# Routing of an attention-then-experts kernel: one product on TensorE, one copy on ScalarE and one merged operation in place of five on GpSimd

## Chip, cores and metric

The kernel runs on one core of a Trainium2 chip. The metric is the device time of one execution in microseconds (us), of which the median of three runs is taken. PE is TensorE's matmul, PEld its weight load, DVE VectorE, ACT ScalarE, POOL GpSimd, SP SyncE.

## What is computed

Four batches of 12288 queries attend to 768 pooled keys each, and each of the 49152 results goes through a gate: a skip score decides whether it is sent to an expert at all, and the largest of eight logits says to which. Cut from the reference:

```python
s = scale * (q @ k.transpose(0, 2, 1))
a = np.exp(s - s.max(-1, keepdims=True)); a /= a.sum(-1, keepdims=True) + 1e-09
x = (a @ v).reshape(B * S, D)
do_compute = x @ w_skip > 0
xc = x[do_compute]
logits = xc @ w_gate
e_idx = np.argmax(logits, axis=1)
gate_w = probs[np.arange(len(xc)), e_idx]        # softmax of the logits
y[mask] = gate_w[mask, None] * (np.maximum(xc[mask] @ w1[e], 0.0) @ w2[e])
out[do_compute] = xc + y
```

## The kernel before, in words

**Two phases.** Phase 1 (until about 1050 us) is attention: 384 tiles of 128 queries, in one loop over t whose order is written out by hand (every engine executes its instructions in the order in which the loop emits them). Phase 2 (from about 1090 us) is the experts, a hardware loop of four steps of 512 rows. Between them a few expert steps are peeled off and woven into the last tiles.

**One tile of phase 1.** TensorE makes the scores of tile t (lines 595 to 597), the weighted sum of tile t-6 (L658) and two transposes of tile t-1 (L633). VectorE takes the row maximum (L603, `nm`), ScalarE the exponential (L608, `p_sb`) and a float16 high part (L612), VectorE the low part (L616). On every second tile VectorE also makes the reciprocal `rs` of the row sums (L666, L668), which empties an accumulator in PSUM that TensorE needs again; ScalarE then scales the rows into the tile `rows` (L673), and SyncE stores them. GpSimd makes the low half of the queries (`q_lo`, L577) and, while batches 0 to 2 run, pools the keys of the batch after (`kvt`, L437 and L440). The last batch has no batch after it, so there these pooling steps are missing.

**Routing.** Every 12 tiles a generator `route` (from L679) is started for the 12x128 rows just finished; 31 of them work for GpSimd (`eng` is GpSimd), and the last 12 tiles are routed in three parts of four tiles by VectorE (`few`). A route is advanced by one step per tile, so its parts lie between the work of the tiles that follow. Its parts, by line:
- L705 to L709: the logits, their maximum and the differences `d`; L721, L722: the position of the maximum; L723: `act`, 1 for a row with a positive skip score; L724, L725: `na`, a large number beyond all rows of the scratch array for an inactive row, 0 for an active one.
- Some tiles later: L733, the exponential `ex` on ScalarE; L735, L737, L738: the one-hot matrix `oh_all` of the chosen expert, with a column of zeros ahead of the 12 tiles of each expert.
- L745: the sum `gs` on VectorE; L765, L766: two products on TensorE into one PSUM tile `misc`, the totals per tile and expert and the counts of the rows above.
- L769: a scan on VectorE, from 0 for each expert, makes running totals `pre` of the 12 tiles; L772 adds the counts inside a tile. On GpSimd L773 makes `nxt`, the totals that the next route starts from, L774 the gate's denominator `gs`, L775 adds the totals `run` that this route started from, L777 selects the expert's column.
- One tile later: L779, VectorE's reciprocal of `gs`, which waits for L774. Then L785, L787: the row number `di`; L788, L789 on GpSimd: the row's scale is copied into column C+2 of `rows`, its number into column C+1; then 12 scatters (L183, one per tile of the route, spread over the tiles that follow) write the rows into the experts' lists in `scr`.

After the last scatter SyncE loads expert rows from `scr` (L189), and phase 2 can begin.

Of the kernel before, what the change touches and what calls it, by code (L numbers as in the profile page):

```python
# [9 lines left out]
F32 = mybir.dt.float32  # L10
# [5 lines left out]
ALU = mybir.AluOpType  # L16
# [4 lines left out]
RT = 12  # L21
# [3 lines left out]
def kernel(  # L25
# [11 lines left out]
    nc = tc.nc  # L37
    NR, C, RT, P = q.shape
# [7 lines left out]
    E, _, FF = w1.shape  # L46
# [32 lines left out]
    BIG = 1 << 20  # L79
# [13 lines left out]
    ones_bf = consts.tile([P, P], BF16, name="ones_bf")  # L93
# [5 lines left out]
    ones_f = consts.tile([P, P], F32, name="ones_f")  # L99
# [10 lines left out]
                            op0=ALU.mult, op1=ALU.add)  # L110
    idt_i = consts.tile([P, RT], I32, name="idt_i")
    nc.gpsimd.iota(idt_i, pattern=[[1, RT]], base=BIG, channel_multiplier=RT)
    idt = consts.tile([P, RT], F32, name="idt")
    nc.gpsimd.tensor_copy(idt, idt_i)

    ends = consts.tile([P, E], F32, name="ends")
# [4 lines left out]
    RTP = RT + 1  # L121
# [44 lines left out]
    op = ctx.enter_context(tc.tile_pool(name="op", bufs=2))  # L166
# [15 lines left out]
    def scatter_rows(dst, ids, src, bound, group):  # L182
        ins = nc.gpsimd.indirect_dma_start(  # L183
            out=dst, out_offset=bass.IndirectOffsetOnAxis(ap=ids, axis=0), in_=src, in_offset=None,
            bounds_check=bound, oob_is_err=False).ins
        return no_dep(ins, group)
# [178 lines left out]
    with ExitStack() as p1:  # L365
# [10 lines left out]
        rt = p1.enter_context(tc.tile_pool(name="rt", bufs=3))  # L376
# [7 lines left out]
        def misc_ps():  # L384
            return ps_m.tile([P, 512], F32, name="misc") if started else acc_ps()
# [161 lines left out]
        accs, scales, snaps = {}, [], []  # L547
# [138 lines left out]
        def route(r, a, b, last, eng):  # L686
            n = b - a
            rows = ROWS[r][:, a:b, :]
            L = rt.tile([P, RT, E], F32, name="lg")[:, 0:n, :]
            S3 = [P, n, E]  # L690
            x_sc = KV[r * RT // TPB][5]

            def small_t(name, dt=F32):
                return rt.tile([P, RT], dt, name=name)[:, 0:n]

            def big_t(name, dt=F32):
                return rt.tile([P, RT, E], dt, name=name)[:, 0:n, :]

            def bc(x):
                return x.unsqueeze(2).broadcast_to(S3)  # L700

            def em(x):
                return x.unsqueeze(1).broadcast_to(S3)

            nc.vector.tensor_tensor(out=L, in0=rows[:, :, C + 1:C + 1 + E], in1=em(gate_ds[:, 1:1 + E]), op=ALU.mult)  # L705
            mx = small_t("mx")
            nc.vector.tensor_reduce(out=mx, in_=L, axis=AX.X, op=ALU.max)
            d = big_t("d")
            eng.tensor_tensor(out=d, in0=L, in1=bc(mx), op=ALU.subtract)  # L709
            ev = big_t("ev")  # L710
            act = small_t("act")
            na = small_t("na")
            few = eng is nc.vector
            if few:
                eng.scalar_tensor_tensor(out=ev, in0=d, scalar=0.0, in1=em(em8), op0=ALU.is_equal, op1=ALU.mult)
                eng.tensor_scalar(out=act, in0=rows[:, :, C], scalar1=0.0, scalar2=None, op0=ALU.is_gt)
                eng.scalar_tensor_tensor(out=na, in0=rows[:, :, C], scalar=0.0, in1=idt[:, 0:n], op0=ALU.is_le,
                                         op1=ALU.mult)
                ohb = oh_few[a // GT % 2]
            else:  # L720
                eng.tensor_scalar(out=ev, in0=d, scalar1=0.0, scalar2=None, op0=ALU.is_equal)  # L721
                eng.tensor_tensor(out=ev, in0=ev, in1=em(em8), op=ALU.mult)  # L722
                eng.tensor_scalar(out=act, in0=rows[:, :, C], scalar1=0.0, scalar2=None, op0=ALU.is_gt)  # L723
                eng.tensor_scalar(out=na, in0=act, scalar1=-1.0, scalar2=1.0, op0=ALU.mult, op1=ALU.add)  # L724
                eng.tensor_tensor(out=na, in0=na, in1=idt[:, 0:n], op=ALU.mult)  # L725
                oha = oh_all[r % 3]
                ohb = oha.rearrange("p e t -> p t e")[:, 1:RTP, :]
            yield
            if not few:
                for _ in range(3 if r < LASTR - 1 else K1):  # L730
                    yield
            ex = big_t("ex")
            nc.scalar.activation(out=ex, in_=d, func=AF.Exp)  # L733
            mn = small_t("mn")
            nc.vector.tensor_reduce(out=mn, in_=ev, axis=AX.X, op=ALU.min)  # L735
            oh = big_t("oh")
            nc.vector.tensor_tensor(out=oh, in0=em(em8), in1=bc(mn), op=ALU.is_equal)  # L737
            eng.tensor_tensor(out=ohb[:, 0:n, :], in0=oh, in1=bc(act), op=ALU.mult)  # L738
            for _ in range(1 if few else 2 if r < LASTR - 1 else K2):
                yield  # L740
            yield (None if r >= LASTR - 1 else GT - 1)
            while accs.get("done", 0) != r * RT + a:
                yield (None if r >= LASTR - 1 else GT - 1)
            gs = small_t("gs")
            nc.vector.tensor_reduce(out=gs, in_=ex, axis=AX.X, op=ALU.add)  # L745
            ps = misc_ps()
            w = n * E
            acc = big_t("acc")
            nxt = ends if last else rt.tile([P, E], F32, name="nxt")
            run = accs.get("run", base0)  # L750
            accs["run"] = nxt
            if few:
                ohf = ohb.rearrange("p t e -> p (t e)")
                nc.tensor.matmul(ps[:, 0:w + E], upper_bf, ohf[:, 0:w + E], start=True, stop=False)
                for j in range(n):
                    nc.tensor.matmul(ps[:, (j + 1) * E:w + E], ones_bf,
                                     ohb[:, j:j + 1, :].broadcast_to([P, n - j, E]), start=False, stop=(j == n - 1))
                nc.vector.tensor_tensor(out=nxt, in0=run, in1=ps[:, w:w + E], op=ALU.add)
                nc.vector.tensor_tensor(out=acc, in0=ps[:, 0:w].rearrange("p (t e) -> p t e", e=E), in1=em(run),
                                        op=ALU.add)  # L760
                nc.vector.tensor_scalar(out=gs, in0=gs, scalar1=1e-9, scalar2=x_sc, op0=ALU.add, op1=ALU.mult)
            else:
                wa = E * RTP
                ohf = oha.rearrange("p e t -> p (e t)")
                nc.tensor.matmul(ps[:, 0:wa], ones_bf, ohf, start=True, stop=True)  # L765
                nc.tensor.matmul(ps[:, wa:2 * wa], upper_bf, ohf, start=True, stop=True)  # L766
                yield
                pre = rt.tile([P, E, RTP], F32, name="pre")
                nc.vector.tensor_tensor_scan(pre.rearrange("p e t -> p (e t)"), keep.rearrange("p e t -> p (e t)"),  # L769
                                             ps[:, 0:wa], 0.0, ALU.mult, ALU.add)  # L770
                inner = ps[:, wa:2 * wa].rearrange("p (e t) -> p t e", t=RTP)[:, 1:RTP, :]
                nc.vector.tensor_tensor(out=acc, in0=inner, in1=pre.rearrange("p e t -> p t e")[:, 0:RT, :], op=ALU.add)  # L772
                eng.tensor_tensor(out=nxt, in0=run, in1=pre[:, :, RT], op=ALU.add)  # L773
                eng.tensor_scalar(out=gs, in0=gs, scalar1=1e-9, scalar2=x_sc, op0=ALU.add, op1=ALU.mult)  # L774
                eng.tensor_tensor(out=acc, in0=acc, in1=em(run), op=ALU.add)  # L775
            accs["done"] = r * RT + b
            eng.tensor_tensor(out=acc, in0=acc, in1=ohb[:, 0:n, :], op=ALU.mult)  # L777
            yield
            nc.vector.reciprocal(rows[:, :, C], gs)  # L779
            yield  # L780
            if r == SNAPR:
                snapshot(accs["run"])
                yield
            dest = small_t("dest")
            nc.vector.tensor_reduce(out=dest, in_=acc, axis=AX.X, op=ALU.add)  # L785
            di = small_t("di", I32)
            nc.vector.tensor_tensor(out=di, in0=dest, in1=na, op=ALU.add)  # L787
            nc.gpsimd.tensor_copy(rows[:, :, C + 2], x_sc.broadcast_to([P, n]))  # L788
            nc.gpsimd.iota(rows.bitcast(I32)[:, :, C + 1], pattern=[[1, n]], base=r * RT * P + a, channel_multiplier=RT)  # L789
            for j in range(n):  # L790
                if j > 0 and r < LASTR - 1 and (j % 2 == 0 or r < SNAPR):
                    yield
                scatter_rows(scr, di[:, j:j + 1], rows[:, j, 0:ROW], E * CAP - 1, "scr")
            if r == SNAPR:
                first_writes.extend(writes)
# [129 lines left out]
        t = -1  # L925
# [138 lines left out]
```

## Time and profile before

| | us |
|---|---|
| median of 3 runs | 1857.39 (1856.57 to 1858.85) |
| the profiled execution, device time | 1859.96 |
| its span, first to last instruction | 1857.0 |
| PE busy | 1752.5 (94%) |
| DVE busy | 1555.6 (84%) |
| ACT busy | 1324.9 (71%) |
| POOL busy | 1144.1 (62%) |
| mean granted clock of TensorE | 0.987 |

The shares are averages over two phases with different limits. Matmuls are pipelined and their ends modelled, so a PE that counts as busy need not be at its peak. "Idle before, releaser" in the rows below is the idle time of an engine ahead of an instruction and what ended it; "issue" is time in which it waited for nothing that the profile shows. Instructions of the sequencers, such as waits and the issue of a DMA, are not counted as busy.

### The profile page before, as it was taken

How to read it: one execution, taken by the hardware profiler on the slowest of the kernel's cores; microseconds unless marked ns; L12 is line 12 of the kernel's file. 1: busy time of each engine (PE TensorE's matmuls, PEld its weight loads, DVE VectorE, ACT ScalarE, POOL GpSimd, SP SyncE). 2: the span in 40 equal slices, each digit the busy share in tenths (PEclk: the TensorE clock that was granted, in tenths of full speed). 3: DMA queues.
4: the chain of work that ended last, by engine and by line, in shares of the span. 5: the costliest groups of instructions: out<-in, count | busy, mean ns of one | idle time of the engine just before them, and what ended most of it. 6: DMA issues, size and time to landing. Idle time of an engine off the chain costs nothing. (4 is left out here: it accounts for less than half of the span.)

```text
span 1857.0 us, 42898 instructions
## 1 busy us (share of the span) xinstructions
PE 1752.5 (94%) x13955; PEld 1260.6 (68%) x13955; DVE 1555.6 (84%) x3226; ACT 1324.9 (71%) x2484; POOL 1144.1 (62%) x1466
## 2 busy tenths in 40 slices
PE   4999999999999999999998879999999999999997
PEld 2998889888889888899998534444444444444443
DVE  7888889988889888998999768887887788778875
ACT  2887788787778787888887546666666666666664
POOL 2378887989978998878778553333333333433343
PEclk9999999999999999999999989999999999999998
DMA  6999999999989999999999443333333333333342
GB/s 179 205 210 201 211 188 216 210 188 175 174 169 198 197 207 204 190 219 221 224 222 188 103 115 98 97 94 93 102 93 94 96 99 93 94 93 102 93 113 73
DMA packets 621971, 284.87 MB, mean 153 GB/s; under 512 B 503168, under 2 KB 571904, under 8 KB 621824
## 3 DMA queue, kind: packets, MB, share of 16 engines
q1 hardware_dynamic: 600320, 244.56, 65.0%
q0 software_dynamic: 21504, 38.43, 6.9%
q8 instruction: 82, 1.34, 0.3%
q14 instruction: 65, 0.53, 0.1%
HBM read 90.60 MB, written 78.64 MB: 91 GB/s over the span
## 5 line engine op out<-in xcount | busy, mean ns | idle before, releaser
L183 POOL DMA_INDIRECT out_dram<-o,xin x288 | 295.3, 1025 | 481.1 <-DVE o L292 414.6
L183 POOL DMA_INDIRECT scr<-rows,di x384 | 413.2, 1076 | 103.3 <-issue 83.3
L269 DVE SCALAR_TENSOR_TENSOR h_lo<-h_ps,h_hi 128x512 f16<-128x512 f32 x544 | 344.2, 686 | 145.8 <-ACT h_hi L268 145.8
L608 ACT ACTIVATE p_sb<-s_ps,nm 128x768 f32<-128x768 f32 x384 | 347.2, 904 | 156.0 <-DVE nm L603 150.4
L603 DVE TENSOR_REDUCE nm<-s_ps 128x1 f32<-128x768 f32 x384 | 363.5, 947 | 54.8 <-PE s_ps L597 53.1
L268 ACT ACTIVATE h_hi<-h_ps 128x512 f16<-128x512 f32 x544 | 318.5, 597 | 51.4 <-PE h_ps L267 31.8
L658 PE MATMUL acc_ps<-v_hi,pt 128*128 128x138 f16 x3072 | 323.2, 225 | 30.3 <-DVE rs L666 30.3
L658 PEld LDWEIGHTS <-pt 128*128 128x128 f16 x4608 | 278.6, 98 | 97.3 <-issue 96.4
L616 DVE SCALAR_TENSOR_TENSOR p<-p_sb,p 128x512 f16<-128x512 f32 x384 | 303.1, 789 | 2.8 <-ACT p L612 2.2
L658 PE MATMUL acc_ps<-v_lo,pt 128*128 128x138 f16 x1536 | 295.9, 224 | 0.0
L595 PE MATMUL s_ps<-k_hi,q_hi 128*128 128x384 f32 x768 | 295.6, 385 | 0.0
L596 PE MATMUL s_ps<-k_lo,q_hi 128*128 128x384 f32 x768 | 261.1, 340 | 0.0
L597 PE MATMUL s_ps<-k_hi,q_lo 128*128 128x384 f32 x768 | 260.2, 339 | 0.0
L612 ACT ACTIVATE p<-p_sb 128x512 f16<-128x512 f32 x384 | 243.2, 633 | 12.6 <-DMA pt<-p 9.3
L265 PE MATMUL h_ps<-xT,w_hi 128*128 128x512 f16 x544 | 206.9, 380 | 8.2 <-issue 8.2
L266 PE MATMUL h_ps<-xT,w_hi 128*128 128x512 f16 x544 | 206.9, 380 | 0.0
L267 PE MATMUL h_ps<-xT,w_lo 128*128 128x512 f16 x544 | 206.7, 380 | 0.0
L281 PE MATMUL y_ps<-h_hi,w_hi 128*128 128x512 f16 x544 | 206.2, 379 | 0.0
L281 PE MATMUL y_ps<-h_hi,w_lo 128*128 128x512 f16 x544 | 206.2, 379 | 0.0
L281 PEld LDWEIGHTS <-w_hi 128*128 128x128 f16 x1152 | 112.7, 98 | 132.6 <-issue 0.7
L284 ACT ACTIVATE yT<-y_ps,y_sc 128x512 f32<-128x512 f32 x68 | 46.8, 688 | 218.3 <-PE y_ps L281 218.3
L281 PE MATMUL y_ps<-h_lo,w_hi 128*128 128x512 f16 x544 | 195.1, 379 | 0.0
(215 smaller groups left out, 3231.3 us busy)
## 6 DMA issues: line engine op xcount, KB each, us to landing
kvt<-in_kv_dram SPq DMA_DIRECT2D x96, 256.0 KB
q_sb<-in_q_dram SPq DMA_DIRECT2D x96, 256.0 KB
out_dram<-rows SPq DMA_DIRECT2D x96, 256.0 KB
xin<-scr SPq DMA_DIRECT2D x75, 264.0 KB, 2.9
w_raw<-in_moe_w_dram SPq DMA_DIRECT2D x38, 512.0 KB, 4.2
scr<-pad SPq DMA_DIRECT2D x32, 264.0 KB
pt<-p SPq DMA_TRANSPOSE x384
scr<-rows,di POOLq DMA_INDIRECT x384
```

The costliest lines, as they stand in the source:

```text
L183: ins = nc.gpsimd.indirect_dma_start(out=dst, out_offset=bass.IndirectOffsetOnAxis(ap=ids, axis=0), in_=src, in_offset=None, bounds_check= ...
L268: nc.scalar.activation(out=h["hi"][:, c, :], in_=ps, func=AF.Relu)
L269: nc.vector.scalar_tensor_tensor(out=h["lo"][:, c, :], in0=ps, scalar=0.0, in1=h["hi"][:, c, :], op0=ALU.max, op1=ALU.subtract)
L281: nc.tensor.matmul(ps, w[:, c, :], h[x][:, c, :], start=(i == 0), stop=(i == len(terms) - 1))
L595: nc.tensor.matmul(s[:, h, :HK], q_hi, k_hi[:, sl], start=True, stop=False)
L596: nc.tensor.matmul(s[:, h, :HK], q_hi, k_lo[:, sl], start=False, stop=False)
L597: nc.tensor.matmul(s[:, h, :HK], q_lo, k_hi[:, sl], start=False, stop=True)
L603: nc.vector.tensor_reduce(out=NM[t], in_=S_PS[t][:, :, :HK], axis=AX.XY, op=ALU.max, negate=True)
L608: nc.scalar.activation(out=P_SB[t], in_=S_PS.pop(t)[:, :, :HK], func=AF.Exp, bias=NM.pop(t))
L612: nc.scalar.activation(out=P16[t][:, 0, :], in_=p_flat(t)[:, 0:KD * P], func=AF.Copy, scale=2.0 ** PEXP)
L616: LO[:] = [nc.vector.scalar_tensor_tensor(out=p16[:, 1, :], in0=p_flat(t)[:, 0:KD * P], scalar=2.0 ** PEXP, in1=p16[:, 0, :], op0=ALU.mult ...
L658: nc.tensor.matmul(ps[:, j % 2, :], w, v[a][:, k, :], start=(i == 0), stop=(i == len(AVL) - 1))
```

## The change

The running totals `run` are no longer added by GpSimd after the scan. A third product on TensorE, one row of ones by one row of eight totals in float32, adds them into the empty column of each expert ahead of the scan, so that `pre` already holds them and its last column is what the next route starts from; L773 and L775 go. `na` becomes one operation with two constants instead of two with a table (an inactive row's number is then the same large constant for all rows). The copy into column C+2 moves from GpSimd, just ahead of the scatters, to ScalarE, just behind `ex`; this one part also holds for the three routes on VectorE.

```diff
                 eng.tensor_scalar(out=act, in0=rows[:, :, C], scalar1=0.0, scalar2=None, op0=ALU.is_gt)
-                eng.tensor_scalar(out=na, in0=act, scalar1=-1.0, scalar2=1.0, op0=ALU.mult, op1=ALU.add)
-                eng.tensor_tensor(out=na, in0=na, in1=idt[:, 0:n], op=ALU.mult)
+                eng.tensor_scalar(out=na, in0=act, scalar1=-float(BIG), scalar2=float(BIG), op0=ALU.mult, op1=ALU.add)
...
             nc.scalar.activation(out=ex, in_=d, func=AF.Exp)
+            nc.scalar.copy(rows[:, :, C + 2], x_sc.broadcast_to([P, n]))
...
-            nxt = ends if last else rt.tile([P, E], F32, name="nxt")
             run = accs.get("run", base0)
-            accs["run"] = nxt
             if few:
+                nxt = ends if last else rt.tile([P, E], F32, name="nxt")
+                accs["run"] = nxt
...
-                nc.tensor.matmul(ps[:, 0:wa], ones_bf, ohf, start=True, stop=True)
+                nc.tensor.matmul(ps[:, 0:wa], ones_bf, ohf, start=True, stop=False)
+                nc.tensor.matmul(ps[:, 0:wa].rearrange("p (e t) -> p e t", t=RTP)[:, :, 0], ones_f[0:1, :], run[0:1, :],
+                                 start=False, stop=True)
                 nc.tensor.matmul(ps[:, wa:2 * wa], upper_bf, ohf, start=True, stop=True)
+                pre = rt.tile([P, E, RTP], F32, name="pre")
+                accs["run"] = pre[:, :, RT]
                 yield
-                pre = rt.tile([P, E, RTP], F32, name="pre")
...
-                eng.tensor_tensor(out=nxt, in0=run, in1=pre[:, :, RT], op=ALU.add)
                 eng.tensor_scalar(out=gs, in0=gs, scalar1=1e-9, scalar2=x_sc, op0=ALU.add, op1=ALU.mult)
-                eng.tensor_tensor(out=acc, in0=acc, in1=em(run), op=ALU.add)
...
             nc.vector.tensor_tensor(out=di, in0=dest, in1=na, op=ALU.add)
-            nc.gpsimd.tensor_copy(rows[:, :, C + 2], x_sc.broadcast_to([P, n]))
             nc.gpsimd.iota(rows.bitcast(I32)[:, :, C + 1], pattern=[[1, n]], base=r * RT * P + a, channel_multiplier=RT)
```

## Rows read from the trace of the kernel before

**Rows 1.** The page, busy tenths of GpSimd in 40 slices of the span.

```profile
POOL 2378887989978998878778553333333333433343
```

**Rows 2.** Stretches of phase 1: PE, PEld, DVE, ACT, POOL busy (count); clock, DMA share, GB/s.

```profile
325.00:516.00 191.00, 177.63 (x1908) 163.67 (x1906) 167.55 (x312) 152.21 (x281) 171.84 (x234) 0.99 0.96 186
828.00:942.00 114.00, 114.00 (x1249) 106.14 (x1247) 104.43 (x208) 99.62 (x184) 92.49 (x124) 1.00 1.14 227
```

**Rows 3.** The scan's line in four stretches: count, ns min/median/max, first and last start.

```profile
L769 DVE TENSOR_TENSOR_SCAN pre<-keep,misc x5: 358/364/364, 130.8 to 259.0; 128x104 f32<-128x104 f32 x5
L769 DVE TENSOR_TENSOR_SCAN pre<-keep,misc x7: 356/357/364, 321.8 to 509.4; 128x104 f32<-128x104 f32 x7
L769 DVE TENSOR_TENSOR_SCAN pre<-keep,misc x7: 357/357/364, 574.9 to 764.1; 128x104 f32<-128x104 f32 x7
L769 DVE TENSOR_TENSOR_SCAN pre<-keep,misc x5: 360/364/365, 826.5 to 941.2; 128x104 f32<-128x104 f32 x5
```

**Rows 4.** Waits of GpSimd from 325 to 516 us: total us, times, longest.

```profile
POOL scr L183 <- issue: 12.6, 65, 0.3
```

**Rows 5.** Waits of GpSimd from 828 to 942 us.

```profile
POOL nxt L773 <- DVE pre L769: 3.9, 4, 1.1
```

**Rows 6.** Waits of all engines from 100 to 950 us.

```profile
PE acc_ps L658 <- DVE rs L666: 23.7, 26, 2.4
DVE rows L779 <- POOL gs L774: 19.6, 13, 2.8
```

**Rows 7.** Timelines of VectorE and TensorE, 417 to 424 us: start, us, idle before.

```profile
419.10 0.23 DVE L779 RECIPROCAL rows<-gs 128x12 f32<-128x12 f32 x1 [1.96 <-POOL gs L774]
...
421.12 0.44 PE L633 MATMUL acc_ps<-ident,p_sb 128*128 128x128 f32 x2 [0.68 <-ACT p_sb L608]
...
423.95 0.39 PE L658 MATMUL acc_ps<-v_hi,pt 128*128 128x138 f16 x2 [1.34 <-DVE rs L666]
```

**Rows 8.** Timeline of GpSimd, 418 to 429 us, around the same route and the next.

```profile
418.47 0.23 POOL L773 TENSOR_TENSOR nxt<-nxt,pre 128x8 f32<-128x8 f32 x1
418.79 0.27 POOL L774 TENSOR_SCALAR gs<-gs,x_sc 128x12 f32<-128x12 f32 x1
419.14 0.39 POOL L775 TENSOR_TENSOR acc<-acc,nxt 128x96 f32<-128x96 f32 x1
419.61 0.43 POOL L777 TENSOR_TENSOR acc<-acc,oh_all 128x96 f32<-128x96 f32 x1
...
423.78 0.21 POOL L788 COPY rows<-x_sc 128x12 f32<-128x12 f32 x1
423.93 0.17 POOL L789 IOTA rows<- 128x12 int32 x1
424.37 1.25 POOL L183 DMA_INDIRECT scr<-rows,di  x1 [0.28 <-POOL rows L789]
...
427.75 0.20 POOL L724 TENSOR_SCALAR na<-act 128x12 f32<-128x12 f32 x1
428.03 0.21 POOL L725 TENSOR_TENSOR na<-na,idt 128x12 f32<-128x12 f32 x1
```

**Rows 9.** Groups of instructions over the span: busy us, mean ns; idle before.

```profile
L765 PE MATMUL misc<-oh_all,ones_bf 128*128 128x104 bf16 x31 | 6.5, 209 | 1.3 <-POOL oh_all L738 1.3
L479 PE MATMUL misc<-dg,ones_f 128*128 128x128 f32 x8 | 2.0, 327 | 0.8 <-DVE dg L475 0.7
L733 ACT ACTIVATE ex<-d 128x32 f32<-128x32 f32 x3 | 0.7, 232 | 0.0
```

**Rows 10.** Timeline of ScalarE, 432 us, the exponential of the route that begins at 421.8 us.

```profile
432.30 0.27 ACT L733 ACTIVATE ex<-d 128x96 f32<-128x96 f32 x1
```

**Rows 11.** Timeline of GpSimd, 859 to 862 us, a route of the last batch.

```profile
859.47 0.66 POOL L788 COPY rows<-x_sc 128x12 f32<-128x12 f32 x1
860.08 0.14 POOL L789 IOTA rows<- 128x12 int32 x1
861.21 1.02 POOL L183 DMA_INDIRECT scr<-rows,di  x1 [0.99 <-POOL rows L789]
```

## The prediction

> **What bounds the kernel now.** I read the page first. Its slices show GpSimd busy eight to nine tenths in the first half and three to four tenths in the second [rows 1]. Routing lies in the first half, so the expert half, where nothing is changed, is left out of the sum. An engine that is busy nine tenths may be a bound or may not; the stretches and waits decide that.
>
> Next the stretches of phase 1. From 325 to 516 us, while keys of a next batch are pooled, TensorE is busy 177.6 of 191 us; from 828 to 942 us, in the last batch, which pools nothing, 114 of 114 us [rows 2]. The scan's starts give the pace, one route per 12 tiles: in the last batch 114.7 us for 4 periods, 28.7 each; in the three stretches with pooling 128.2 us for 4, 187.6 for 6 and 189.2 for 6, together 505.0 us for 16 periods, 31.56 each [rows 3]. So 16 periods of 31 are each 2.9 us longer than attention needs, 45.8 us in all.
>
> Who is at fault is seen in GpSimd's waits. From 325 to 516 us it is busy 171.8 us and spends 12.6 us in the issue gaps ahead of its scatters; the 6.6 us left of the 191 are gaps of at most 0.3 us, such as the 0.09 us between L773 and L774 [rows 2, 4, 8]. It never waits for another engine for long: it runs its queue without a rest, and the 31 to 32 us of a period are its own work. In the last batch it waits for the scan in each of four routes, 3.9 us in all [rows 5]. So GpSimd **is the bound of the 16 periods**, although its share of the span is only 62%.
>
> The waits of the others show how this reaches TensorE: VectorE's reciprocal L779 stands in its queue until GpSimd has made `gs`, 19.6 us in 13 times, and TensorE waits for VectorE's `rs`, 23.7 us [rows 6]. In one route: L779 starts at 419.10 after 1.96 us of idle VectorE; behind it in the queue stand the row maximum and `rs`, so TensorE idles 0.68 us for `p_sb` and 1.34 us for `rs` [rows 7].
>
> **The change part by part.** For a bound engine the price of an instruction is the distance of its start to that of the next, and it is paid in each of the 16 periods.
> - L773: 418.47 to 418.79, 0.32 us; L775: 419.14 to 419.61, 0.47 us; one of the two `na` operations: 427.75 to 428.03, 0.28 us; the copy L788: 423.78 to 423.93, 0.15 us [rows 8]. Together 1.22 us per period. 16 times that is **19.5 us**. What is late next: GpSimd still, as 31.56 - 1.22 = 30.3 us stays above 28.7; no floor takes the gain away.
> - In the first pooling route of each of three batches GpSimd starts without a lag and has to build one up before it hurts. I take half the price there, 3 x 0.6 = **1.8 us**; the ends are 0 and 3.7.
> - `gs` no longer stands behind L773, so it also loses the wait for the scan; this is in the 0.32 us. Where GpSimd waits for the scan today [rows 5], in the last batch, the end gains nothing: VectorE does not wait there.
> - The end of phase 1: TensorE waits once 1.3 us for GpSimd's `oh_all` [rows 9]; with the L775, copy and `na` of the route before gone, 0.9 us of that goes. The three last routes have a copy of 0.15 us ahead of their number and scatters, 0.45 us in a chain that the last load waits for. Together **1.3 us**; ends 0 and 1.8.
> - Added to TensorE: 31 float32 products of 8 columns. No row shows one. The lower end is 0, hidden in the idle time of the 16 periods; the upper is the 0.33 us of a float32 product of 128 columns [rows 9] in all 31, 10.2 us. I take 0.15, under half of the upper one, as the columns are a sixteenth; it is hidden in the 16 periods (cover: the 23.7 us of waits [rows 6]) and paid in 15: **+2.2 us**. Its input, the last column of the route before, is a period old, so it adds no wait.
> - Added to ScalarE: 34 copies of up to 12 elements a row. The nearest row, 32 elements a row, takes 0.23 us [rows 9]. Cover: ScalarE is idle 38.8 of 191 us and 14.4 of 114 us [rows 2], some 3.6 us a period at least. I take 0. Without cover 7.8 us. Behind it in ScalarE's queue stand the high parts and the next exponential. No DMA is added, removed or moved past another.
>
> The sum is -19.5 - 1.8 - 1.3 + 2.2 = -20.4 us. The profiled execution took 1859.96 us, 3.0 us of it around its span, so it would take 1839.6; it stands 2.6 us above the median, and from the median the sum gives **1837 us**. About 0.2%, 3.7 us, is what a measurement of this kernel can tell from no change.
>
> **The rivals.**
> - *GpSimd gets slower as it catches up.* When it runs without a lag, its small operations meet other work: in the last batch the copy takes 0.66 us in place of 0.21, and from the start of L789 to its scatter pass 1.13 us in place of 0.44 [rows 8, 11]. If periods with pooling came to look like that, 0.69 us of the 1.22 would be given back: 16 x 0.53 = 8.5 us, sum -9.4, **1848 us**. Against it: with 30.3 us of work GpSimd keeps a lag. By the Trainium skill (SBUF — State Buffer, "Who interferes with whom") a VectorE instruction with two SBUF inputs and a GpSimd instruction that reads SBUF exclude each other, and the one that came later is blocked to the other's end. The copy's two durations agree with such blocking, and by this rule alone freed time on GpSimd is not safely gained: the sum would come out nearer to 1848 than to 1837. Chance 0.12.
> - *The stall goes altogether.* If a smaller lag no longer reached VectorE, the 16 periods would fall to 28.7 us: -45.8 - 1.3 + 2.2, **1812 us**. Against it stands that GpSimd would have to lose 2.9 us a period and loses 1.22. Chance 0.05.
> - *Nothing is gained.* That VectorE waits for `gs` is inferred from semaphores; if the scatters' own pace held the queue (12.6 us of issue gaps, [rows 4]), fewer operations between them would leave the period as it is: -1.3 + 2.2, **1858 us**. Against it: L773 to L777 follow each other with no scatter between them [rows 8]. Chance 0.07.
> - *Slower: ScalarE's copy waits.* It writes a column of `rows` that VectorE and GpSimd read at the start of the route. If it had to wait for GpSimd's last reading, ScalarE's queue would be held as VectorE's is now, about the 0.68 + 1.34 = 2.0 us of TensorE's idle time in [rows 7] for each of 16 routes: +32 - 20.4, **1869 us**. It decides when GpSimd's reading, ahead of L724 at 427.75, ends later than `ex` at 432.30 [rows 8, 10]: there are 4.5 us between, and a smaller lag widens them. Chance 0.06.
>
> **How the numbers follow.** The forecast has 0.70: 1837 us, its own range 1829 to 1846 (low with all of the edge routes and no cost on TensorE, and some contention less; high with the full 10.2 us on TensorE). Rivals 0.12, 0.05, 0.07 and 0.06. The range that leaves out no more than 0.2 is 1828 to 1849: it takes in the first rival and leaves out the other three, 0.18. Faster: 0.70 + 0.12 + 0.05 and a little of the third, 0.87; same 0.07; slower 0.06.
>
> **What would show it.** Right: scans 30.3 us apart on average in the three stretches and still 28.7 to 28.9 in the last batch; GpSimd still without waits from 325 to about 510 us; VectorE's wait at L779 for `gs` down from 19.6 us to under 10, TensorE's for `rs` below 15; 31 float32 products close to 0.1 to 0.2 us of TensorE's time; ScalarE's copy near 0.2 us with no idle time ahead of it; phase 2 as long as before, only earlier. Wrong: scans further apart than 31 us, GpSimd's other operations longer by what was removed, or idle time of ScalarE ahead of its copy.

## The result, and the profile after

The kernel after takes 1842.24 us (median of 6 runs, 1838.59 to 1847.69), the kernel before, in 6 runs beside it, 1859.64 us. The ratio is 0.9908, with an interval of 0.9894 to 0.9923: 17.1 us less, where 20.4 was forecast. A second set of runs, after_again, on another chip, gave 1844.52 us and 0.991 (0.989 to 0.993). The profiled execution of after took 1847.69 us (span 1845.2), the slowest of its six; that of after_again 1844.5 (span 1841.9). So both traces are read below.

| | after, us | share of the span |
|---|---|---|
| PE busy | 1757.6 | 95% |
| DVE busy | 1549.4 | 84% |
| ACT busy | 1325.3 | 72% |
| POOL busy | 1104.0 | 60% |
| mean granted clock | 0.992 | |

The page of after, GpSimd's busy tenths, which answer to [rows 1]:

```profile
POOL 2369887889968998766767543333333333333333
```

The first half still has its eights and nines. The starts of the scan in the four stretches of [rows 3] give the pace (its line is L772 now):

```profile
L772 DVE TENSOR_TENSOR_SCAN pre<-keep,misc x5: 356/357/364, 134.1 to 258.8; 128x104 f32<-128x104 f32 x5
L772 DVE TENSOR_TENSOR_SCAN pre<-keep,misc x7: 354/357/363, 322.0 to 504.7; 128x104 f32<-128x104 f32 x7
L772 DVE TENSOR_TENSOR_SCAN pre<-keep,misc x7: 355/357/360, 568.2 to 752.4; 128x104 f32<-128x104 f32 x7
L772 DVE TENSOR_TENSOR_SCAN pre<-keep,misc x5: 360/362/363, 815.6 to 932.8; 128x104 f32<-128x104 f32 x5
```

The 16 periods with pooling take 124.7 + 182.7 + 184.2 = 491.6 us, 30.7 each, where 505.0 stood before. The last batch went the other way: 117.2 us for four periods, 29.3 each, against 114.7. The whole span, cut at the scans (31 of them) of three traces, with the forecast's terms put where they belong (0.15 us of product in each of 15 routes):

| stretch | before | after | after_again | forecast of the difference |
|---|---|---|---|---|
| start to the first scan | 101.9 | 104.5 | 104.6 | +0.2 |
| 16 periods with pooling | 505.1 | 491.6 | 488.5 | -19.5 |
| 4 periods that begin a batch | 113.8 | 116.6 | 116.1 | -1.2 |
| 3 periods that end one | 105.8 | 102.9 | 104.4 | +0.4 |
| last batch, 4 periods | 114.6 | 117.2 | 116.2 | +0.6 |
| last 3 periods of GpSimd's routes | 94.7 | 92.5 | 92.5 | -0.9, with the next |
| from there to the end | 821.1 | 819.9 | 819.7 | |
| span | 1857.0 | 1845.2 | 1841.9 | -20.4 |

So the gain lies in the 16 periods, as forecast, but is 13.5 to 16.6 us instead of 19.5. The periods that begin a batch and those of the last batch have become longer, and the time to the first scan too. Two traces of one kernel differ by 3 us in the 16 periods here, and by 6 us in t2 below; a difference of that size between two traces says nothing.

The stretches that answer to [rows 2], same columns; the third is a short one near the start:

```profile
322.00:505.00 183.00, 176.25 (x1898) 161.87 (x1897) 167.09 (x314) 151.44 (x284) 163.72 (x207) 1.00 1.04 194
816.00:930.00 114.00, 113.63 (x1235) 104.89 (x1234) 101.45 (x202) 97.92 (x185) 81.49 (x107) 1.00 1.16 222
47.40:50.80 3.40, 3.40 (x19) 3.09 (x20) 2.58 (x5) 2.65 (x5) 0.28 (x1) 0.50 1.41 150
```

GpSimd still runs without a rest while it pools: 163.7 of 183 us busy, and of its waits there 11.6 us are issue gaps of the scatters. In the last batch TensorE is as busy as ever (113.6 of 114 us), so its periods can have grown only by work of its own. The third line is taken up at the end.

Waits of after from 100 to 950 us (us in total, times, longest), which answer to [rows 6], and one that is new:

```profile
PE acc_ps L658 <- DVE rs L666: 12.7, 17, 1.2
DVE rows L780 <- POOL gs L776: 11.8, 9, 2.5
POOL acc L778 <- DVE acc L775: 19.3, 11, 2.6
```

TensorE's wait for `rs` has halved (23.7 to 12.7), VectorE's for `gs` fell from 19.6 to 11.8. The third wait lies almost wholly outside the 16 periods: in the last batch and where a batch begins, GpSimd makes `gs` ahead of the scan now and then waits for VectorE's `acc`, in the last batch in the place of its wait at L773.

### The profile page after: what moved, and what is told of

Read it like the earlier page. It is cut to its first block, busy times and chain, and to the rows that moved or that the text cites. A ratio compares the mean times of both kernels' runs of the same rounds, so it can differ in the third digit from the quotient of the medians.

```text
span 1845.2 us, 42946 instructions
## 1 busy us (share of the span) xinstructions
PE 1757.6 (95%) x14017; PEld 1263.0 (68%) x14017; DVE 1549.4 (84%) x3226; ACT 1325.3 (72%) x2518; POOL 1104.0 (60%) x1339
## 5 line engine op out<-in xcount | busy, mean ns | idle before, releaser
L616 DVE SCALAR_TENSOR_TENSOR p<-p_sb,p 128x512 f16<-128x512 f32 x384 | 298.1, 776 | 4.2 <-ACT p L612 3.6
```

Source lines behind the costliest of these rows:

```text
L616: LO[:] = [nc.vector.scalar_tensor_tensor(out=p16[:, 1, :], in0=p_flat(t)[:, 0:KD * P], scalar=2.0 ** PEXP, in1=p16[:, 0, :], op0=ALU.mult ...
```

## The experiments

The theory: in the 16 periods GpSimd's queue is the bound, so that each of its instructions costs its own time there, and the product costs TensorE time wherever TensorE is the bound. The rivals: only the place of `gs` in GpSimd's queue matters, not the amount of work; the freed time is given back as other GpSimd work gets longer; the product is hidden. Each run differs from the kernel before or after by the edit shown. "16 periods" and "last batch" are worked out from the scans as above.

**The parts by themselves.** t1_totals_alone has the new product and neither L773 nor L775, with `na` and the copy as before; t2_na_and_copy_alone has the other two parts and no product. t2_again is the same kernel as t2, run later on another chip.

```diff
 # t2, against before
-                eng.tensor_scalar(out=na, in0=act, scalar1=-1.0, scalar2=1.0, op0=ALU.mult, op1=ALU.add)
-                eng.tensor_tensor(out=na, in0=na, in1=idt[:, 0:n], op=ALU.mult)
+                eng.tensor_scalar(out=na, in0=act, scalar1=-float(BIG), scalar2=float(BIG), op0=ALU.mult, op1=ALU.add)
...
+            nc.scalar.copy(rows[:, :, C + 2], x_sc.broadcast_to([P, n]))
...
-            nc.gpsimd.tensor_copy(rows[:, :, C + 2], x_sc.broadcast_to([P, n]))
```

> The kernel before with the running totals brought in by the float32 product on TensorE, L773 and L775 gone, but with two operations for na and the copy on GpSimd as before. Theory A (GpSimd bounds the 16 periods with pooling, and the product costs TensorE the 0.41 us by which its neighbours stand further apart, wherever TensorE is the bound): GpSimd saves 16 x 0.79 = 12.6 us, the product costs 15 x 0.41 = 6.2 us, together 6 to 7 us faster than before; scans of the last batch 29.0 us apart. Theory B (the product is hidden, the missing gain was given back by GpSimd): about 8 us faster, scans of the last batch 28.7 us apart.

> The kernel before with na made in one operation and the copy on ScalarE, the running totals as before. Theory A: GpSimd saves 16 x 0.43 = 6.9 us and 1 us at the end of phase 1, TensorE has nothing added: 7 to 8 us faster than before, scans of the last batch 28.7 us apart as before. A rival, ScalarE's copy costs the tile behind it its 0.21 us: scans of the last batch 28.9 us apart, and 6 us less gain. Theory B: 3 us faster or less.

> na in one operation and the copy on ScalarE once more, for a second trace. The first run gave 0.9958 of before, but its trace shows the 16 periods unchanged (505.6 us). Theory A: the 16 periods together are 498 us (505 less 16 x 0.43), and the first trace was a slow draw. Theory B: again near 505 us, the gain lies outside them.

Measured: t1 1850.51 us, 0.9952 (0.9936 to 0.9968); 16 periods 490.4, last batch 116.1. t2 1854.21, 0.9958 (0.994 to 0.9975); t2_again 1853.17, 0.9967 (0.9957 to 0.9977); 16 periods 505.6 and 499.6 in their profiles. The scans of t1 in the last batch:

```profile
L772 DVE TENSOR_TENSOR_SCAN pre<-keep,misc x5: 361/362/364, 817.0 to 933.1; 128x104 f32<-128x104 f32 x5
```

So t1 has both faces of the change: 14.6 us shorter periods with pooling, 2 us more than their price of 12.6, and a last batch at 29.0 us a period, as after. Its 9.4 us by the medians are more than the 6 to 7 expected. t2 gains 5.8 and 6.7 us by the medians, near its price of 16 x 0.43 = 6.9, and leaves the last batch at 28.6. But only its second trace shows a gain in the 16 periods; the first has them as long as before, so where t2's gain lies is not shown. The two gains, 9.4 and about 6 us, nearly add up to the 17 of the whole.

**Na alone, the copy alone.** t8_na_alone and t9_copy_alone are the two halves of t2.

> The kernel before with na in one operation alone. Theory A: 16 x 0.28 = 4.5 us faster. Theory B: within 2 us of before.

> The kernel before with the copy of the scale on ScalarE alone. Theory A: 16 x 0.15 = 2.4 us in the periods and 0.5 us at the end of phase 1, 3 us faster; scans of the last batch 28.7 us apart. Rival (ScalarE's copy costs the tile behind it): 28.9 us in the last batch and no gain.

Measured: t8 1857.79 us, 0.9989 (0.9976 to 1.0003), 16 periods 506.6; t9 1860.45, 1.0005 (0.9995 to 1.0014), 16 periods 507.0. The price of t8 is 16 x 0.28 = 4.5 us, which its interval just reaches, while its median gains 2.0; the price of t9 is 16 x 0.15 = 2.4 us, which its interval (0.9 us less to 2.6 more) leaves out. In their profiles the 16 periods are no shorter than the 505.0 of before. What is longer instead can be read in `q_lo`, GpSimd's most frequent instruction next to the scatters: its groups from 130 to 755 us (busy us, mean ns), of before, after, t8 and t9:

```profile
L577 POOL TENSOR_TENSOR q_lo<-q_sb,q_hi 128x256 fp32r<-128x256 f32 x119 | 99.3, 835 | 8.1 <-PE misc L523 5.5 <-DVE p L616 1.8
```

```profile
L577 POOL TENSOR_TENSOR q_lo<-q_sb,q_hi 128x256 fp32r<-128x256 f32 x121 | 104.3, 862 | 9.8 <-PE misc L523 5.4 <-DVE p L616 1.8
```

```profile
L577 POOL TENSOR_TENSOR q_lo<-q_sb,q_hi 128x256 fp32r<-128x256 f32 x118 | 105.7, 895 | 9.8 <-PE misc L523 5.5 <-DVE p L616 1.8
```

```profile
L577 POOL TENSOR_TENSOR q_lo<-q_sb,q_hi 128x256 fp32r<-128x256 f32 x118 | 102.0, 865 | 8.2 <-PE misc L523 5.5 <-DVE p L616 1.8
```

In t8 the same work takes 60 ns more each, 118 x 0.060 = 7.1 us over the stretch, more than the 4.5 that were removed; in t9 30 ns, 3.5 us, against 2.4. That is the way in which the first rival saw the gain go back. But the mean of `q_lo` moves between 835 and 916 ns from version to version (916 in t6 below, which removes nothing); what sets it is read from the timelines in the next section. That the pair gains some 6 us where the halves gain 2 us and nothing is still within the intervals: they leave t8 up to 4.5 us of gain and t9 up to 0.9, and the pair in t2_again as little as 4.3. t9's last batch keeps 28.6 us a period, so ScalarE's copy costs nothing there.

**The order in the queue.** t6_gate_first is the kernel before with `gs` ahead of L773, so that `gs` no longer stands behind the wait for the scan; no work is removed.

```diff
-                eng.tensor_tensor(out=nxt, in0=run, in1=pre[:, :, RT], op=ALU.add)
                 eng.tensor_scalar(out=gs, in0=gs, scalar1=1e-9, scalar2=x_sc, op0=ALU.add, op1=ALU.mult)
+                eng.tensor_tensor(out=nxt, in0=run, in1=pre[:, :, RT], op=ALU.add)
```

> The kernel before with L774 moved ahead of L773, nothing removed: VectorE's reciprocal waits 0.32 us less for GpSimd, whose work is the same. Theory A (GpSimd's work per period is the bound): no more than 1 us faster than before, 0.32 us in each of three batches, within 0.2%. Rival (the order on GpSimd, not the amount of its work, made the wait): VectorE's wait for gs falls by 13 x 0.32 = 4 us and the kernel is 4 us or more faster.

Measured: 1863.3 us, 1.0008 (0.9994 to 1.0023); 16 periods 507.9. Its wait for `gs` from 100 to 950 us:

```profile
DVE rows L779 <- POOL gs L773: 24.6, 12, 3.6
```

VectorE waits for `gs` no less than the 19.6 us of [rows 6]. The place in the queue gives nothing: `gs` is late because GpSimd is late with everything. That rival falls.

**The product alone.** t3_product_alone is the kernel before with a float32 product of the same shape ahead of the second product, into eight columns of the PSUM tile that nothing reads.

```diff
+                nc.tensor.matmul(ps[:, 2 * wa:2 * wa + E], ones_f[0:1, :], run[0:1, :], start=True, stop=True)
                 nc.tensor.matmul(ps[:, wa:2 * wa], upper_bf, ohf, start=True, stop=True)
```

> The kernel before with a float32 product of one row by eight columns added between the two products of every GpSimd route, into columns that nothing reads. Theory A: 15 x 0.41 = 6 us slower than before; scans of the last batch 29.1 us apart in place of 28.7, those of the stretches with pooling 31.5 as before. Theory B: no change, 28.7 us in the last batch.

Measured: 1865.37 us, 1.0028 (1.0018 to 1.0038), 5.2 us more than before; 16 periods 503.4, no longer than before. Its scans in the last batch, to be held against the last line of [rows 3]:

```profile
L770 DVE TENSOR_TENSOR_SCAN pre<-keep,misc x5: 360/363/364, 833.9 to 950.1; 128x104 f32<-128x104 f32 x5
```

116.2 us for four periods against 114.7: the product costs 0.4 us in each route in which TensorE is the bound, and nothing that shows where GpSimd is.

**The totals without a product.** t4_totals_by_scalar is the kernel after, with the totals copied by ScalarE into the empty columns, behind both products. after_again and t4_again are after and t4, run together on one chip.

```diff
-                nc.tensor.matmul(ps[:, 0:wa].rearrange("p (e t) -> p e t", t=RTP)[:, :, 0], ones_f[0:1, :], run[0:1, :],
-                                 start=False, stop=True)
                 nc.tensor.matmul(ps[:, wa:2 * wa], upper_bf, ohf, start=True, stop=True)
+                nc.scalar.copy(ps[:, 0:wa].rearrange("p (e t) -> p e t", t=RTP)[:, :, 0], run)
```

> The changed kernel with the product taken out and the totals written into the empty columns by a copy of ScalarE (128 x 8, float32, into PSUM) behind the products. Theory A: TensorE gets its 0.41 us back in the routes where it is the bound: 6 us faster than the changed kernel, about 23 us faster than before, scans of the last batch 28.7 us apart. Theory B: the same as the changed kernel, 17 us faster than before.

> The changed kernel itself, for the comparison on one chip: ratio to before 0.989 to 0.992; a product costs its route 0.41 us, scans of the last batch 29.0 us apart.

> The kernel of t4 once more, beside the changed kernel on the same chip. Theory A (the product's 0.41 us count in the 15 routes without pooling): 6 us faster than the changed kernel. If the earlier near-tie of the medians was right: within 3 us.

Measured: t4 1841.0 us, 0.9899 (0.9879 to 0.9919); t4_again 1841.8, 0.9895 (0.9875 to 0.9915); 16 periods 489.5 and 490.5, last batch 114.5, as before the change. The profiled spans are 1836.9 and 1837.6 us, against 1845.2 and 1841.9 of after. By the medians the gain over after is 1 to 3 us, where 6 were expected, and the intervals overlap, so what taking the product away gives is shown in the routes of the last batch and only probable in the whole time.

**More of the same.** t5_gate_by_scalar_too is t4 with `gs` scaled by ScalarE instead of GpSimd, which leaves out the 1e-9 added to the sum. t10_number_early is t5 with the row numbers (L789) made right behind the exponential, well before the scatters instead of just ahead of them.

```diff
 # t5, against t4
-                eng.tensor_scalar(out=gs, in0=gs, scalar1=1e-9, scalar2=x_sc, op0=ALU.add, op1=ALU.mult)
+                nc.scalar.activation(out=gs, in_=gs, func=AF.Copy, scale=x_sc)
 # t10, against t5
             nc.scalar.copy(rows[:, :, C + 2], x_sc.broadcast_to([P, n]))
+            nc.gpsimd.iota(rows.bitcast(I32)[:, :, C + 1], pattern=[[1, n]], base=r * RT * P + a, channel_multiplier=RT)
...
-            nc.gpsimd.iota(rows.bitcast(I32)[:, :, C + 1], pattern=[[1, n]], base=r * RT * P + a, channel_multiplier=RT)
```

> The kernel of t4 with the gate's denominator also scaled by ScalarE, as soon as VectorE has summed it, in place of GpSimd's L774 (the 1e-9 is left out, which changes nothing in float32 as the sum is at least 1). GpSimd loses another 0.35 us per route and VectorE's reciprocal no longer waits for GpSimd at all; its next wait for GpSimd is at the sum of acc, a tile later. Theory A (GpSimd's queue sets the pace): 16 x 0.35 = 5.6 us less, and about 2 us of lag more that each of three batches may carry, so 6 to 10 us faster than the kernel of t4. Theory B (what is removed from GpSimd is mostly given back): within 3 us of t4.

> The kernel of t5 with the iota for the row numbers (L789) moved from just ahead of the scatters to the place of ScalarE's copy, some tiles earlier, so that the first scatter no longer waits for it. Theory A (GpSimd's queue sets the pace in the 16 periods): the 0.28 us of idle GpSimd ahead of the first scatter goes in each, 16 x 0.28 = 4.5 us faster than t5. Theory B (what GpSimd gets back is lost again to collisions with VectorE): within 2 us of t5.

Measured: t5 1832.39 us, 0.9842 (0.9819 to 0.9865), 16 periods 482.3; t10 1827.29 us, 0.9828 (0.9812 to 0.9845), 16 periods 477.5. Scans of t10 in the three stretches with pooling and, from 797.0 us, in the last batch:

```profile
L772 DVE TENSOR_TENSOR_SCAN pre<-keep,misc x5: 357/364/367, 132.3 to 251.1; 128x104 f32<-128x104 f32 x5
L772 DVE TENSOR_TENSOR_SCAN pre<-keep,misc x7: 355/362/367, 313.5 to 492.8; 128x104 f32<-128x104 f32 x7
...
L772 DVE TENSOR_TENSOR_SCAN pre<-keep,misc x5: 362/365/367, 797.0 to 911.5; 128x104 f32<-128x104 f32 x5
```

29.8 us a period, still above the 28.6 of the last batch. From 100 to 950 us GpSimd's scatters wait for VectorE's logits, a wait that is not among those of before or after:

```profile
POOL scr L183 <- DVE lg L705: 26.4, 23, 2.4
```

Of it only 3.3 us, in 11 waits of at most 0.3, lie in the 16 periods, so there GpSimd's queue is still the bound. t10 beats both kernels: its interval lies wholly below that of after. Over t5 its gain is 5.1 us by the medians and 2.6 by the ratios, and the intervals overlap, so that step is probable and not shown.

## Why the prediction was right, and where its terms were not

The forecast was 1837 us, the range 1828 to 1849; 1842.24 lies in it, 5.2 us above the forecast, on the side to which the first rival pulled. 2.2 us of that are the starting point, as before took 1859.64 us in the runs beside it and not 1857.39; by the medians the change gained 3.0 us less than the sum. That it is no more is in part luck: several terms below missed by 2 to 6 us, most of them to the same side, and the two profiled executions gained only 11.8 and 15.1 us of span.

**The bound.** That GpSimd's queue sets the 16 periods holds. GpSimd's busy time in them, summed over the three stretches from first to last scan, of before and after:

```profile
sum 505.00, POOL 455.07; mean POOL 151.69
sum 491.60, POOL 441.75; mean POOL 147.25
```

It is idle for 49.9 us in both, as 505.0 - 455.1 and 491.6 - 441.8 give. In the same stretches of the other twelve traces its idle time lies between 45.7 us (t10) and 52.3 us (t6), while its busy time runs from 431.8 to 456.7 us: the periods are as long as GpSimd's work. t6 changes the order and gains nothing. The seven traces of kernels with L773 and L775 have 499.6 to 507.9 us for the 16 periods, the five of after, t1 and t4 have 488.5 to 491.6, and t5 and t10, which take more out or move it, 482.3 and 477.5. Not every removed instruction shows: t1 keeps the copy and both `na` operations, and its 490.4 us are no more than the 491.6 and 488.5 of after. From the last scan of GpSimd's routes to the end it takes 819.9 us instead of 821.1, so phase 2 is only moved, as expected.

**-19.5, the 16 periods: 13.5 and 16.6 in the two traces.** The term was mis-sized, in two ways. First, a price from start to start holds the gap behind an instruction. Of the 1.22 us in [rows 8], 0.25 are such gaps, 4.0 us in 16 periods, and they were not gained: GpSimd's idle time is 49.9 us before, 49.9 in after and 50.0 in after_again. One part of what came in their place is the first scatter's wait for the row number, 4.5 us before and 5.7 in both traces of after. Second, the work that is left does not keep its length. The removed instructions themselves fill 0.23 + 0.39 + 0.20 + 0.15 = 0.97 us a period, 15.5 us, and the busy time fell by 13.3 us in after and 16.7 in after_again. In after `q_lo` takes 862 ns in place of 835, 121 x 0.027 = 3.3 us more; in after_again its mean is 837. GpSimd's timeline of after, around one route:

```profile
440.12 1.20 POOL L577 TENSOR_TENSOR q_lo<-q_sb,q_hi 128x256 fp32r<-128x256 f32 x1
...
443.77 0.75 POOL L577 TENSOR_TENSOR q_lo<-q_sb,q_hi 128x256 fp32r<-128x256 f32 x1
...
447.04 0.27 POOL L776 TENSOR_SCALAR gs<-gs,x_sc 128x12 f32<-128x12 f32 x1
447.39 0.45 POOL L778 TENSOR_TENSOR acc<-acc,oh_all 128x96 f32<-128x96 f32 x1
```

The first two lines are one operation of one shape, 1.20 us and 0.75 us. What tells them apart is an instruction of VectorE with two inputs:

```profile
439.42 1.32 DVE L616 SCALAR_TENSOR_TENSOR p<-p_sb,p 128x512 f16<-128x512 f32 x1
```

It was running, until 440.74, when the first `q_lo` began, and that `q_lo` ended 0.58 us behind it; no L616 ran when the second began. The timelines of all 14 traces from 130 to 755 us say the same. 435 `q_lo` took 1.13 to 1.28 us, and every one of them began while an L616 ran (to within 0.01 us). The other 1247 took 0.78 us at most, and none of them did, but for six that began within 0.011 us of its start. The mean of `q_lo` thus tells how many fall on an L616: 23 of 119 before, 31 of 121 in after, 25 of 122 in after_again, 39 of 118 in t8, 44 of 118 in t6. The rule of the Trainium skill (SBUF — State Buffer, "Who interferes with whom") is that a VectorE instruction with two inputs from SBUF and a GpSimd instruction that reads SBUF block each other; these traces agree, with 1.20 us against 0.75. So the collision behind the first rival is real, but it did not come from a queue that catches up: t6 removes nothing and has the most. The rival would have given back 0.69 of 1.22 us a period; what the traces are short of the price, gaps included, is (19.5 - 13.5) / 16 = 0.38 and (19.5 - 16.6) / 16 = 0.18. The last two lines of GpSimd's timeline are all that is left of the four that stand at this place in [rows 8].

**+2.2, the product: mis-sized, and its upper bound with it.** The timeline of TensorE in one route of after:

```profile
841.36 0.21 PE L765 MATMUL misc<-oh_all,ones_bf 128*128 128x104 bf16 x1
841.49 0.39 PE L766 MATMUL misc<-pre,ones_f 1*128 1x8 f32 x2
841.81 0.22 PE L768 MATMUL misc<-oh_all,upper_bf 128*128 128x104 bf16 x1
841.85 0.42 PE L595 MATMUL s_ps<-k_hi,q_hi 128*128 128x384 f32 x1
```

and in the same place of before:

```profile
823.63 0.21 PE L765 MATMUL misc<-oh_all,ones_bf 128*128 128x104 bf16 x1
823.68 0.21 PE L766 MATMUL misc<-oh_all,upper_bf 128*128 128x104 bf16 x1
823.71 0.42 PE L595 MATMUL s_ps<-k_hi,q_hi 128*128 128x384 f32 x1
```

From the first product to the next tile's scores it was 0.08 us and is 0.49: the new product costs 0.41 us, not 0.15, and the bound of 0.33 was too low as well. The step that failed is the reading of the float32 row in [rows 9]: L479 stands there with x8, yet its line runs once for each of four batches. A float32 product is two instructions, and 0.33 us was half of one. The groups of after say the same for the new line (count, then busy us and mean ns):

```profile
L766 PE MATMUL misc<-pre,ones_f 1*128 1x8 f32 x60 | 11.5, 262 | 0.0
L766 PEld LDWEIGHTS misc<-pre,ones_f 1*128 1x128 f32 x60 | 8.8, 183 | 5.6 <-issue 1.3
L765 PE MATMUL misc<-oh_all,ones_bf 128*128 128x104 bf16 x31 | 6.5, 209 | 1.1 <-POOL oh_all L738 1.1
L765 PEld LDWEIGHTS <-ones_bf 128*128 128x128 bf16 x31 | 3.0, 98 | 0.0
L733 ACT COPY rows<-x_sc 128x12 f32<-128x12 f32 x31 | 6.6, 214 | 0.0
```

60 for 30 products (the first route's two stand in a row of their own), each with its own weight load of 183 ns, nearly twice the 98 of a bfloat16 one; two weight loads are 0.37 us, most of the 0.41, so taking the columns as a scale was the wrong choice. The Trainium skill (TensorE: Matmul & The Clock Gate, "Weight-path perf modes") says that the fast weight load is not used for float32; the 183 against 98 ns agree in their direction. With 15 routes the term is 15 x 0.41 = 6.2 us; t3 measured 5.2 as a whole. The cover in the 16 periods held: t3 lengthens none of the three stretches by more than 0.2 us.

**-1.8, the first periods of a batch: wrong sign.** 113.8 became 116.6 and 116.1 us for the four. There GpSimd has no lag, so its lighter queue gains nothing (the lower end, 0): t4, without the product, has 113.9 and 113.6. The product makes them longer, by more than its 4 x 0.41 = 1.6 us: t3 has 117.5. What the rest is was not found.

**-1.3, the end of phase 1: not shown.** The last three periods and what follows went from 915.8 to 912.4 and 912.2 us, -3.4 and -3.6, product included. But the two traces of t2, one kernel, have 912.8 and 915.7, and t6, which removes nothing, has 914.2, so a difference of this size against one trace of before does not size the term.

**0, ScalarE's copy: right.** 214 ns each, no idle time ahead of it (the last line of those groups), so the rival of the waiting copy did not happen. The stall did not go altogether either, and that nothing is gained is refuted by t1.

**What would show it.** TensorE's wait for `rs` fell below 15 as expected; VectorE's for `gs` only to 11.8, not below 10; the scans are 30.7 and 30.5 us apart, not 30.3; the last batch at 29.3 and 29.0 lies outside the 28.7 to 28.9, by the product.

## What to carry to other kernels

An engine at 62% of the span can be the bound of a stretch; there an instruction taken from it is worth about its own time; the gap behind it was not gained here, and its other instructions grow longer or shorter as they fall on another engine's or miss them. So a price worked out from single rows is an estimate: t1 gained 14.6 us for 12.6, after 13.5 and 16.6 for 19.5. Work moved from that engine is not free on another that bounds the neighbouring stretches: look up there how the operation is executed, and set a row's count against how often its line runs, as the two together tell into how many instructions one call falls. The cheapest place for a handful of elements was ScalarE, which had idle time in every stretch: t10 is 32 us faster than before, nearly twice the change's gain, by going there with two more operations and by moving a third to where the queue had room.

## What the runs showed of the hardware that had not been expected

**A small float32 product costs nearly as much as a large one.** 8 columns took 262 ns an instruction, two instructions a product, against 326 ns for 128 columns in before.

**Two engines in each other's way.** A `q_lo` of GpSimd that begins while VectorE's L616 runs takes 1.2 us in place of 0.75, in every one of 435 cases.

**A slow stretch ahead of the first route.** From 47.4 to 50.8 us TensorE's granted clock is 0.50 in after, the lower of its two levels, 1.2 GHz (the third line of the stretches of after above), and 0.51, 0.53 and 0.64 on average in after_again, t3 and t1, the other three traces with the product. In before, and in the other nine without it, it is 1.00:

```profile
47.40:50.80 3.40, 3.40 (x39) 3.08 (x38) 2.83 (x5) 3.40 (x7) 0.53 (x1) 1.00 1.32 121
```

39 matmuls run in those 3.40 us, 19 in after. In the 3.4 us ahead of it TensorE was busy 2.26 us in before and 1.62 us in after. The first scan starts at 103.6 to 104.8 us in the four traces and at 100.2 to 103.3 us in the ten. Yet the first product belongs to the first route, just ahead of that scan and tens of us behind the dip, so why TensorE idles longer before it is open; nothing was tried on it by itself.
